# Moving loads, transforms and small matmuls between the steps of a fused Fourier-mixing and MLP kernel

## The chip, the cores and the metric

The kernel runs on one core of a Trainium2 chip. The metric is device time in microseconds (us), as the median of several executions. The granted clock is the share of TensorE's full clock that the profile shows as granted; 0.5 is called half clock here. Engines: PE is TensorE (PEld its weight loads), DVE is VectorE, ACT is ScalarE, POOL is GpSimd, and SP is SyncE, here used only to issue DMAs. Ratios are the mean time of one kernel's fast runs over the mean of the other's fast runs of the same rounds, so they are not quite the ratio of the medians quoted beside them. Verdicts are given at 2%.

## The reference

```python
# x: (8, 3008, 256) float32; w_in: (256, 2048); w_out: (2048, 256)
X = np.fft.fft(x, axis=1)          # along the sequence
X = np.fft.fft(X, axis=2).real     # along the channels, real part kept
h = X.reshape(24064, 256) @ w_in
out = (h * np.cos(h)) @ w_out
```

## The kernel before

The channel transform is folded into `w_in` once. The sequence transform of each batch is made of matmuls against constant matrices, after DVE has folded the 3008 rows by symmetry. Its result goes into ring buffers `Rr`, `Ir` and `Rb`. The MLP runs over 47 column tiles of 8 steps each, 376 steps in all; a batch lasts 47 steps. In each step PE makes `pp` and `pq` from the rings, DVE and ACT make `h`, and two steps later PE multiplies `h` into `po`. All other work (loads of the next batch, its folds, its transforms) is hung on steps by `at(step, fn)`.

Channel 128 of batches 1 to 7 is treated apart, which I call the one-channel stage. Two gathers fetch it, element by element, and seven batches are transformed together:

```python
    X0, X1 = Rr[0 : NB - 1, HALF + 32 :], Ir[0 : NB - 1, HALF + 32 :]

    def load_ext():                                  # the two gathers
        with nc.allow_non_contiguous_dma(reason="one channel"):
            for t, row in ((X0, 0), (X1, SEQ - 1536)):
                nc.sync.dma_start(
                    out=t,
                    in_=bass.AP(tensor=xt, offset=x.offset + (SEQ + row) * ND + 128,
                                ap=[[SEQ * ND, NB - 1], [ND, 1536], [1, 1]]))
```

A transform is six matmul instructions into two PSUM tiles, and a function that evacuates them with one ACT copy and two or three DVE operations:

```python
    def dft_pair(ri, kodd, stat, width, M, low, high, mid, banks=("da", "db")):
        pa = dps(banks[0])
        pb = dps(banks[1])
        # ... 3 matmuls into pb, 3 into pa ...
        def evacuate():
            bs = spool.tile([128, NE], FP, tag="bs", bufs=2, name="bs")
            pin(nc.scalar.copy(out=bs[0:M, 0:n], in_=pb[0:M, 0:n]))
            # ... DVE: sum and difference of bs and pa into the ring ...
        return evacuate
```

The schedule (`pin` keeps an operation in program order; everything else is ordered by the builder's scheduler):

```python
    at(2, lambda: dft_R(0, 1, EO)())          # matmuls and evacuation in one step
    at(5, lambda: dft_I(0, 1, EO)())
    at(8, lambda: dft_first(1, xb)())
    if NB > 1:
        at(1, load_ext)
        at(22, lambda: dft_ext(1, NB - 1, fold_ext()))   # whole one-channel stage
    for b in range(1, NB):
        s0 = (b - 1) * steps_b                            # steps_b = 47
        at(s0 + 1, lambda b=b: start_batch(b))            # issues the x loads
        for i in range(20):
            at(s0 + 5 + i, lambda i=i: state["ops"][FOLDS[i]]())
        at(s0 + 26, lambda b=b: dft_R(b, 0, state["EO"])())
        # ... dft_I at +29, dft_R at +32, dft_I at +35, spread_ext at +30 ...
    at(last - 8, spread4)
    at(last, middle_tokens)     # the 8 middle rows: 16 matmuls of 8 columns, MLP, 16 more
```

## Time and profile before

| | before |
|---|---|
| median (7 runs) | 2170.89 us |
| lowest, highest | 2168.28, 2178.56 us |
| profiled execution (not one of the 7) | 2167.05 us, span of the core 2165.3 us |
| PE, DVE, ACT busy | 99%, 84%, 41% |

These are lines of the page of the kernel before: the span, engine busy times with their share and count, the rows of PE's busy tenths and of the granted clock in 40 slices of 54 us, and the first line of the chain that ended last (the work that the end of the span waited for, followed back step by step).

```profile
span 2165.3 us, 24330 instructions
PE 2135.6 (99%) x9576; PEld 1809.5 (84%) x9576; DVE 1818.4 (84%) x2520; ACT 893.8 (41%) x896; POOL 109.6 (5%) x100
PE   8799999999999999999999999999999999999999
PEclk9899999999999999999999999999999999999999
PE 69%; DVE 21%; ACT 5%; DMA 1%; issue 1%; DVEq 0%; ACTq 0%
```

PE's 99% alone doesn't tell how much is to be won, since its passes overlap (those of `po` last 380 ns in the mean and start 216 ns apart) and a pass at half clock counts as busy all the same (four of them for 2.08 us below). I therefore used the start times of the passes. Each fp32 matmul instruction shows up as two passes, and a pass of 256 columns starts 216 ns after the one before it in the undisturbed stretches. What lies above that spacing (317 ns for 377 columns) is lost PE time. Summed per form it was 42 us in this execution. The largest piece, 18.4 us, lies between 76 and 99 us.

The PE timeline of the kernel before there (columns: start, length, engine, line, operation, tiles, shapes, count, and in brackets the idle time before with what ended it):

```profile
73.45 3.62 PE L555 MATMUL po<-w,h 128*128 128x256 f32 x16
87.92 2.08 PE L483 MATMUL pp<-Rr,Wc 128*128 128x256 f32 x4 [10.85 <-DVE pt L502]
89.78 1.91 PE L492 MATMUL pq<-Ir,Ws 127*128 127x256 f32 x4
```

Four passes took 1.03 us elsewhere and take 2.08 and 1.91 us here: after the gap the clock is at half (0.50 granted from 82.37 to 99.44 us). Here is the DVE instruction that ended the gap, from the timeline of all engines:

```profile
86.92 0.17 DVE L251 COPY e<-xl 128x6 f32<-128x6 f32 x1 [17.58 <-DMA xl<-in_x_dram]
```

`pt` stands behind this copy, the first fold of batch 1, in DVE's order, and starts right after it, at 87.00 us. And this is the queue of SyncE in the same stretch, where a length is that of the issuing instruction:

```profile
25.65 0.98 SPq L432 DMA_DIRECT2D Rr<-in_x_dram  x1
26.68 32.95 SPq L432 DMA_DIRECT2D Ir<-in_x_dram  x1
59.75 21.71 SPq L138 DMA_DIRECT2D xl<-in_x_dram  x1
81.56 0.37 SPq L140 DMA_DIRECT2D xl<-in_x_dram  x1
```

The gathers (`Rr` and `Ir` are their targets) stand ahead of the x tile (`xl`), and its issue isn't over until 81.5 us. The waits view of the kernel before (who waited for whom: us in total, times, longest):

```profile
DVE pt L502 <- PE pp L483: 38.5, 63, 3.9
PEld po L555 <- DVE h L534: 18.6, 42, 3.4
PE po L555 <- DVE h L534: 5.6, 9, 2.7
```

Last, the PE timeline of the one-channel stage of the kernel before:

```profile
189.45 5.50 PE L461 MATMUL da<-ident,Rr 7*128 7x7 f32 x24
195.26 3.62 PE L310 MATMUL db<-MC,xe 128*7 128x377 f32 x6 [0.32 <-ACT xe L469]
198.71 2.07 PE L310 MATMUL da<-MC,xe 128*7 128x377 f32 x6
```

Six passes of 377 columns took 3.62 us and then 2.07 us: the first six ran at half clock (0.50 granted from 191.60 to 198.43 us), right after 24 tiny passes.

### The profile page before, as it was taken

The numbers are of one execution on the slowest core, as the hardware profiler recorded it, in microseconds if no ns is written. First come the engines' busy times: TensorE is split into PE (matmuls) and PEld (weight loads), VectorE is DVE, ScalarE is ACT, GpSimd is POOL, SyncE is SP. The second block draws the span as 40 slices with busy tenths as digits, with TensorE's granted clock in tenths as the row PEclk, the third lists the DMA queues.
The fourth block names the chain that finished last, engine by engine and source line by source line (L and its number), as shares of the span: only waits on it lengthen the run. The fifth ranks groups of instructions, "written<-read, shape, count | busy, mean of one in ns | idle before, by whom it ended". The sixth has DMA issues, their size and how long they took to land.

```text
span 2165.3 us, 24330 instructions
## 1 busy us (share of the span) xinstructions
PE 2135.6 (99%) x9576; PEld 1809.5 (84%) x9576; DVE 1818.4 (84%) x2520; ACT 893.8 (41%) x896; POOL 109.6 (5%) x100
## 2 busy tenths in 40 slices
PE   8799999999999999999999999999999999999999
PEld 4587888888888888888888888888888888888887
DVE  5598788997889978898789987899778997888877
ACT  2243344443444434444344444444344443444434
POOL 4011000110001100010000200011000000000000
PEclk9899999999999999999999999999999999999999
DMA  8511000110011100110001100011000000000000
GB/s 255 46 35 41 25 10 24 54 34 11 10 40 40 35 10 10 53 36 24 10 10 58 47 10 11 23 56 32 10 10 25 20 10 10 10 17 14 10 11 20
DMA packets 63234, 66.02 MB, mean 30 GB/s; under 512 B 29576, under 2 KB 55944, under 8 KB 62607
## 3 DMA queue, kind: packets, MB, share of 16 engines
q1 hardware_dynamic: 56446, 51.86, 8.2%
q0 software_dynamic: 4608, 12.59, 2.1%
q8 instruction: 76, 1.25, 0.3%
q10 hardware_dynamic: 2066, 0.02, 0.1%
q14 instruction: 38, 0.31, 0.0%
HBM read 39.75 MB, written 24.69 MB: 30 GB/s over the span
## 4 chain that ended last, share of the span: by engine, by line
PE 69%; DVE 21%; ACT 5%; DMA 1%; issue 1%; DVEq 0%; ACTq 0%
PE po L555 43%; PE pp L483 10%; PE pq L492 10%; DVE r L528 6%; DVE h L534 5%; DVE pt L502 3%; ACT r L525 3%; DVE h L511 3%; DVE h L512 3%; PE db L310 2%; PE da L310 2%; DMA xl<-in_x_dram 1%; ACT r L531 1%; DVE o L238 1%; DVE e L238 0%
## 5 line engine op out<-in xcount | busy, mean ns | idle before, releaser
L555 PE MATMUL po<-w,h 128*128 128x256 f32 x6016 | 1366.7, 380 | 5.6 <-DVE h L534 5.6
L555 PEld LDWEIGHTS po<-w,h 128*128 128x128 f32 x6016 | 1138.8, 190 | 177.4 <-DVE h L534 18.6
L525 ACT ACTIVATE r<-h 128x1024 int32<-128x1024 f32 x377 | 396.9, 1053 | 626.9 <-DVE h L512 622.9
L531 ACT ACTIVATE r<-r,halfpi 128x1024 f32<-128x1024 f32 x377 | 432.4, 1147 | 540.9 <-DVE r L528 540.9
L528 DVE TENSOR_TENSOR r<-h,r 128x1024 f32<-128x1024 f32 x377 | 460.0, 1220 | 165.8 <-ACT r L525 162.6
L534 DVE SCALAR_TENSOR_TENSOR h<-h,r 128x1024 f32<-128x1024 f32 x377 | 459.2, 1218 | 53.0 <-ACT r L531 51.6
L483 PE MATMUL pp<-Rr,Wc 128*128 128x256 f32 x1504 | 390.6, 380 | 10.8 <-DVE pt L502 10.8
L492 PE MATMUL pq<-Ir,Ws 127*128 127x256 f32 x1504 | 388.9, 379 | 0.0
L502 DVE SCALAR_TENSOR_TENSOR pt<-Rb,wex,pp 128x256 f32<-128x256 f32 x752 | 330.7, 475 | 38.9 <-PE pp L483 38.5
L483 PEld LDWEIGHTS pp<-Rr,Wc 128*128 128x128 f32 x1504 | 285.9, 190 | 55.9 <-DVE pt L502 11.3
L492 PEld LDWEIGHTS pq<-Ir,Ws 127*128 127x128 f32 x1504 | 285.6, 190 | 41.1
L511 DVE TENSOR_TENSOR h<-pt,pq 128x512 f32<-128x512 f32 x376 | 258.0, 686 | 33.8 <-DVE pt L502 0.9
L512 DVE TENSOR_TENSOR h<-pt,pq 128x512 f32<-128x512 f32 x376 | 255.7, 680 | 0.0
L130 POOL DMA_INDIRECT xl<-in_x_dram,ix x96 | 109.4, 1140 | 1389.2 <-DVE o L238 1345.5
L576 ACT COPY ob<-po 128x512 f32<-128x512 f32 x94 | 54.3, 578 | 52.6 <-PE po L555 52.1
L310 PE MATMUL db<-MC,eo 128*128 128x377 f32 (+3 forms) x186 | 65.0, 486 | 2.0 <-DVE eo L238 2.0
L310 PE MATMUL da<-MC,eo 128*128 128x377 f32 (+3 forms) x186 | 64.7, 483 | 0.0
L310 PEld LDWEIGHTS da<-MC,eo 128*128 128x128 f32 (+1 forms) x186 | 35.7, 192 | 24.4 <-issue 1.2
L310 PEld LDWEIGHTS db<-MC,eo 128*128 128x128 f32 (+1 forms) x186 | 35.4, 191 | 20.4 <-DVE eo L238 2.8
L251 DVE COPY e<-xl 128x6 f32<-128x6 f32 x32 | 5.4, 167 | 33.1 <-DMA xl<-in_x_dram 33.1
L238 DVE TENSOR_TENSOR o<-xl 128x762 f32<-128x762 f32 x32 | 30.3, 948 | 0.0
L238 DVE TENSOR_TENSOR e<-xl 128x762 f32<-128x762 f32 x32 | 30.3, 946 | 0.0
(65 smaller groups left out, 218.4 us busy)
## 6 DMA issues: line engine op xcount, KB each, us to landing
out_dram<-ob SPq DMA_DIRECT2D x158, 128.0 KB
xl<-in_x_dram SPq DMA_DIRECT2D x16, 768.0 KB
MC<-dft_mats SPq DMA_DIRECT2D x4, 1131.0 KB
Rb<-r SPq DMA_DIRECT2D x4, 752.0 KB
h<-in_moe_w_in_dram SPq DMA_DIRECT2D x4, 512.0 KB
w<-in_moe_w_out_dram SPq DMA_DIRECT2D x1, 2048.0 KB
xl<-in_x_dram,ix POOLq DMA_INDIRECT x96
out_dram<-ob SPq DMA_DIRECT2D x10, 112.0 KB
```

What stands on the lines that cost most here:

```text
L130: nc.gpsimd.indirect_dma_start(out=L[j][:, m * ND : (m + 1) * ND], out_offset=None, in_=xflat, in_offset=bass.IndirectOffsetOnAxis(ap=ix[: ...
L310: nc.tensor.matmul(ps[0:M, 0:n], lhsT=stat[:, m * width : m * width + M], rhs=MC[ri, kodd][:, c : c + n], start=(t == 0), stop=(t == 2),)
L483: nc.tensor.matmul(pp[:, i * TW : (i + 1) * TW], lhsT=Wc[:, f * 128 : (f + 1) * 128], rhs=Rr[:, pos : pos + TW], start=True, stop=True,)
L492: nc.tensor.matmul(pq[:, i * TW : (i + 1) * TW], lhsT=Ws[0:127, f * 128 : (f + 1) * 128], rhs=Ir[:, pos : pos + TW], start=True, stop=True,)
L502: nc.vector.scalar_tensor_tensor(out=pt[:, i * TW : (i + 1) * TW], in0=Rb[:, pos : pos + TW], scalar=wex[:, f : f + 1], in1=pp[:, i * TW : ...
L511: nc.vector.tensor_tensor(out=h[:, 0:512], in0=pt, in1=pq, op=ALU.add)
L512: nc.vector.tensor_tensor(out=h[:, 512:1024].rearrange("p (f c) -> p f c", f=2)[:, :, ::-1], in0=pt.rearrange("p (f c) -> p f c", f=2), in ...
L525: nc.scalar.activation(out=k, in_=h[:, 0:n], func=AF.Copy, bias=0.25, scale=1.0)
L528: nc.vector.tensor_tensor(out=r[:, 0:n], in0=h[:, 0:n], in1=k, op=ALU.subtract)
L531: nc.scalar.activation(out=r[:, 0:n], in_=r[:, 0:n], func=AF.Sin, bias=halfpi, scale=TWO_PI)
L534: nc.vector.scalar_tensor_tensor(out=h[:, 0:n], in0=h[:, 0:n], scalar=TWO_PI, in1=r[:, 0:n], op0=ALU.mult, op1=ALU.mult,)
L555: nc.tensor.matmul(T.po[sg][:, gr * ND : (gr + 1) * ND], lhsT=g[:, c : c + 128], rhs=w2[:, f * ND : (f + 1) * ND], start=(f == 0 and gr == 0),
```

## The change

The intent is to take lumps out of the schedule. There are five parts:

1. The gathers are issued after the x tiles of batch 1 (step 2 instead of 1, and pinned).
2. Folds and transforms of all batches come two steps later.
3. Each transform is evacuated one step after its matmuls.
4. The one-channel stage is cut into a fold, four pieces of transposes, and two transforms three steps apart.
5. The 16 small matmuls of the middle tokens are spread, two to a step.

The diff, cut to its core:

```diff
     def load_ext():
 ...
-                nc.sync.dma_start(
+                pin(
+                    nc.sync.dma_start(
 ...
+    def at_dft(step, fn):
+        def first():
+            state["evacuate"] = fn()
+        at(step, first)
+        at(step + 1, lambda: state["evacuate"]())
 ...
-    at(2, lambda: dft_R(0, 1, EO)())
+    at_dft(2, lambda: dft_R(0, 1, EO))
 ... (the same at 5 and 8)
-        at(1, load_ext)
-        at(22, lambda: dft_ext(1, NB - 1, fold_ext()))
+        at(2, load_ext)
+        at(21, fold_ext)
+        for part in range(4):
+            at(22 + part, lambda part=part: turn_ext(part))
+        at_dft(30, lambda: dft_ext(0))
+        at_dft(33, lambda: dft_ext(1))
+        at(34, store_ext)
 ...
-        for i in range(20):
-            at(s0 + 5 + i, lambda i=i: state["ops"][FOLDS[i]]())
-        at(s0 + 26, lambda b=b: dft_R(b, 0, state["EO"])())
+        for i, key in enumerate(FOLDS):
+            at(s0 + 7 + i, lambda key=key: state["ops"][key]())
+        at_dft(s0 + 28, lambda b=b: dft_R(b, 0, state["EO"]))
 ... (the same for 29, 32, 35 -> 31, 34, 37; spread_ext two steps later, five for batch 1)
+    for part in range(8):
+        at(last - 8 + part, lambda part=part: middle_first(part))
     at(last, middle_tokens)
```

More of the change, by code (lines that the diff above doesn't have):

```diff
@@ L183 @@
     wex = cpool.tile([128, NF], FP, tag="wex")
+    state = {}
     Rr = cpool.tile([128, RING], FP, tag="Rr")
@@ L389, in dft_I, with dft_ext, low, high @@
         return dft_pair(1, kodd, EO[2 + kodd], 127, 127, low, high, None, **kw)
-    def dft_ext(b0, nb, ext):
-        rx = spool.tile([NB, HALF], FP, tag="xl3", bufs=1, name="rx")
-        rx4 = spool.tile([NB, 1], FP, tag="rx4", bufs=1, name="rx4")
-        for kodd in range(2):
-            def low(op, a, z, kodd=kodd):
-                op(rx[0:nb, kodd * RUN + a : kodd * RUN + z], a, z)
-            def high(op, a, z, kodd=kodd):
-                top = kodd * RUN + (RUN - 1 if kodd else RUN)
-                op(rx[0:nb, top - a : top - z : -1], a, z)
-            dft_pair(
-                0, kodd, ext[kodd], nb, nb, low, high,
-                lambda hi: hi(rx4[0:nb, :], 0, 1),
-            )()
-        nc.sync.dma_start(out=r128_dr[b0 : b0 + nb, :], in_=rx[0:nb, :])
+    def dft_ext(kodd):
+        nb = NB - 1
+        if kodd == 0:
+            state["rx"] = spool.tile([nb, HALF], FP, tag="xl3", bufs=1, name="rx")
+            state["rx4"] = spool.tile([nb, 1], FP, tag="rx4", bufs=1, name="rx4")
+        rx, rx4 = state["rx"], state["rx4"]
+        def low(op, a, z):
+            op(rx[:, kodd * RUN + a : kodd * RUN + z], a, z)
+        def high(op, a, z):
+            top = kodd * RUN + (RUN - 1 if kodd else RUN)
+            op(rx[:, top - a : top - z : -1], a, z)
+        return dft_pair(
+            0, kodd, state["ext"][kodd], nb, nb, low, high,
+            lambda hi: hi(rx4, 0, 1),
+        )
+    def store_ext():
+        nc.sync.dma_start(out=r128_dr[1:NB, :], in_=state["rx"])
         nc.sync.dma_start(
-            out=r4_dr[:, b0 : b0 + nb].rearrange("o b -> b o"), in_=rx4[0:nb, :]
+            out=r4_dr[:, 1:NB].rearrange("o b -> b o"), in_=state["rx4"]
         )
@@ L431, in load_ext @@
             for t, row in ((X0, 0), (X1, SEQ - 1536)):
-                nc.sync.dma_start(
-                    out=t,
-                    in_=bass.AP(
-                        tensor=xt,
-                        offset=x.offset + (SEQ + row) * ND + 128,
-                        ap=[[SEQ * ND, NB - 1], [ND, 1536], [1, 1]],
-                    ),
+                pin(
+                    nc.sync.dma_start(
+                        out=t,
+                        in_=bass.AP(
+                            tensor=xt,
+                            offset=x.offset + (SEQ + row) * ND + 128,
+                            ap=[[SEQ * ND, NB - 1], [ND, 1536], [1, 1]],
+                        ),
+                    )
                 )
@@ L455, in fold_ext, with turn_ext @@
         pin(nc.vector.memset(em[:, n:768], 0.0))
+    def turn_ext(part):
         nb = NB - 1
-        ps = dps("da")
-        for i, t in enumerate((ep, em)):
-            for m in range(6):
-                c = (i * 6 + m) * nb
-                pin(nc.tensor.matmul(
-                    ps[:, c : c + nb],
-                    lhsT=t[:, m:768:6],
-                    rhs=ident[0:nb, 0:nb],
-                    start=True,
-                    stop=True,
-                ))
+        ep, em = X0[:, 0:768], X0[:, 768:1536]
+        if part == 0:
+            state["xe_ps"] = dps("da")
+        ps = state["xe_ps"]
+        for j in range(3 * part, 3 * part + 3):
+            i, m = divmod(j, 6)
+            pin(nc.tensor.matmul(
+                ps[:, j * nb : (j + 1) * nb],
+                lhsT=(ep, em)[i][:, m:768:6],
+                rhs=ident[0:nb, 0:nb],
+                start=True,
+                stop=True,
+            ))
+        if part < 3:
+            return
         xe = spool.tile([128, 12 * nb], FP, tag="xe", bufs=1, name="xe")
         pin(nc.scalar.copy(out=xe, in_=ps[:, 0 : 12 * nb]))
-        return [xe[:, 0 : 6 * nb], xe[:, 6 * nb :]]
+        state["ext"] = [xe[:, 0 : 6 * nb], xe[:, 6 * nb :]]
     class Tile:
@@ L599, in store, with middle_first @@
                 j += n
-    def middle_tokens():
-        pm = dps("da")
-        for f in range(NF):
+    def middle_first(part):
+        if part == 0:
+            state["pm"] = dps("da")
+        pm = state["pm"]
+        for f in range(2 * part, 2 * part + 2):
             nc.tensor.matmul(
@@ L611, in middle_tokens @@
             )
+    def middle_tokens():
+        pm = state["pm"]
         n = NF * NB
@@ L660 @@
     steps_b = HALF * 8 // TW
-    state = {}
+    def at_dft(step, fn):
[3 more added lines that the diff above has]
+        at(step + 1, lambda: state["evacuate"]())
     def start_batch(b):
         state["EO"], state["ops"] = fold_x(load_x(b))
-    at(2, lambda: dft_R(0, 1, EO)())
-    at(5, lambda: dft_I(0, 1, EO)())
-    at(8, lambda: dft_first(1, xb)())
+    at_dft(2, lambda: dft_R(0, 1, EO))
+    at_dft(5, lambda: dft_I(0, 1, EO))
+    at_dft(8, lambda: dft_first(1, xb))
     if NB > 1:
-        at(1, load_ext)
-        at(22, lambda: dft_ext(1, NB - 1, fold_ext()))
+        at(2, load_ext)
[5 more added lines that the diff above has]
+        at(34, store_ext)
     for b in range(1, NB):
@@ L674 @@
         at(s0 + 1, lambda b=b: start_batch(b))
-        for i in range(20):
-            at(s0 + 5 + i, lambda i=i: state["ops"][FOLDS[i]]())
-        at(s0 + 26, lambda b=b: dft_R(b, 0, state["EO"])())
-        at(s0 + 29, lambda b=b: dft_I(b, 0, state["EO"])())
-        at(s0 + 32, lambda b=b: dft_R(b, 1, state["EO"])())
-        at(s0 + 35, lambda b=b: dft_I(b, 1, state["EO"])())
-        at(s0 + 30, lambda b=b: spread_ext(b))
+        for i, key in enumerate(FOLDS):
+            at(s0 + 7 + i, lambda key=key: state["ops"][key]())
+        at_dft(s0 + 28, lambda b=b: dft_R(b, 0, state["EO"]))
+        at_dft(s0 + 31, lambda b=b: dft_I(b, 0, state["EO"]))
+        at_dft(s0 + 34, lambda b=b: dft_R(b, 1, state["EO"]))
+        at_dft(s0 + 37, lambda b=b: dft_I(b, 1, state["EO"]))
+        at(s0 + (35 if b == 1 else 32), lambda b=b: spread_ext(b))
     total = n_tiles * 8
```

## The prediction

> **What bounds the kernel now.** TensorE. The busy table gives PE 99% of 2165.3 us, DVE 84%, ACT 41%. In the timeline most steps repeat every 5.18 us, which is 24 passes, so one starts every 216 ns. Start-to-start time above the median of a pass's own form sums, over all 9576 passes, to only 42 us of lost PE time: 8.4 us in the first 40 us, 18.4 us between 76 and 99 us, about 3 us between 189 and 199 us, and 12 us in pieces of 0.2 to 0.7 us. Only those can be won by moving work; no engine gets more instructions.
>
> **The large gap.** The waits view has one DVE wait of 17.58 us, ending at 86.92 us: the first copy of the batch-1 fold, on the landing of the x tile. The SyncE queue shows why: the two one-channel gathers (7 x 1536 elements of 4 bytes each) are issued at 25.65 and 26.68 us, the second issue lasts 32.95 us, and that of the x tile behind it 21.71 us. [...] from 55 to 80 us some 2500 four-byte packets per 5 us pass, and next to no bytes. Behind it PE idles 10.85 us (pp waits for pt) and 2.73 us (po for h), and the granted clock is 0.5 from 82.4 to 99.4 us, costing the remaining 4.8 us. [...]
>
> **What the change does there.** The x tiles of batch 1 now stand ahead of the gathers on the queue, and the folds start two steps (10 us) later. The x issue should come near 35 us, when its buffer comes free, and land by 50 to 60 us; the first fold wants it near 75 us. The gathers, some 55 us long (estimate from this trace), are wanted only at step 21 (about 150 us). So the DVE wait, the PE gap and the slow clock go: -18.4 us, all on the critical path.
>
> **The one-channel stage.** Before: 24 tiny transposes (5.5 us) and four transforms run in one block at 189 to 204 us; PE waits 0.46 + 0.32 us, the clock is 0.5 from 191.6 to 198.4 us and six passes take 0.63 us instead of 0.32. Spread out, the clock should stay at 1: -3 us. The 5.5 us of transposes stay.
>
> **The rest.** Splitting each transform from its evacuation frees ACT waits (3.7 us at most) that PE hardly feels: 0 to -2 us. The middle-token matmuls (3.5 us) only move: 0. In fold steps DVE has about 5.7 us of work per 5.18 us step; the 5 us of one-channel folding at step 21 now has less PE work right behind it to let DVE catch up: up to +2 us of new PE waits.
>
> **Sum.** -18.4 - 3 - 1 + 1 = -21: predicted 2149 us, range 2141 to 2158. Chances: faster by over 2% (2127.5, more than all avoidable loss) 0.01, within 2% 0.98, slower 0.01.
>
> **What would show it.** Right: no DVE wait above 3 us on the x tile after 40 us; no idle PE near 76 to 92 us; clock digits 9 in the second to fourth slice; span near 2144. Wrong: if the gathers still delay the x tile or the first output stores (ACT waits for an output buffer near 120 us); if DVE falls behind at 150 to 180 us and PE waits there for h; if a transform waits over 1 us for the evacuation of the last (single buffers).

## The result and the profile after

| | before | after |
|---|---|---|
| median | 2170.89 us (15 runs) | 2142.39 us (6 runs) |
| lowest, highest | 2165.78, 2178.80 us | 2140.79, 2144.34 us |
| span of the profiled execution | 2165.3 us | 2140.7 us |
| ratio, 95% interval | | 0.9863 [0.9847, 0.988] |

The change is 1.4% faster. Two things in the table need an explanation beyond the median: the scatter shrank from 13 us to 3.6 us, and the medians lie 28.5 us apart but the profiled spans only 24.6 us. The lines of the page that answer to those of before:

```profile
span 2140.7 us, 24296 instructions
PE 2126.8 (99%) x9576; PEld 1807.6 (84%) x9576; DVE 1821.0 (85%) x2520; ACT 893.6 (42%) x896; POOL 111.0 (5%) x100
PE   8999999999999999999999999999999999999999
PEclk9999999999999999999999999999999999999999
PE 98%; DVE 1%; POOL 0%; DMA 0%; issue 0%; ACT 0%; DVEq 0%; ACTq 0%
```

PE does the same 9576 passes, but the chain that ended last now runs over PE for 98% of the span, where it ran over DVE for 21% before. The SyncE queue of the changed kernel:

```profile
34.76 0.36 SPq L138 DMA_DIRECT2D xl<-in_x_dram  x1
35.22 0.37 SPq L140 DMA_DIRECT2D xl<-in_x_dram  x1
35.64 0.97 SPq L440 DMA_DIRECT2D Rr<-in_x_dram  x1
36.66 27.70 SPq L440 DMA_DIRECT2D Ir<-in_x_dram  x1
96.32 0.82 SPq L611 DMA_DIRECT2D out_dram<-ob  x2
```

The first output stores are issued at 96.32 us, after the gathers (99% of their packets had started by 86.5 us), so they aren't held up either.

The first fold of batch 1 finds its data without a wait, and PE, in its own timeline of the changed kernel, goes on through that stretch at full speed (four passes in 1.03 us):

```profile
83.49 0.17 DVE L253 COPY e<-xl 128x6 f32<-128x6 f32 x1
```

```profile
77.89 1.03 PE L499 MATMUL pp<-Rr,Wc 128*128 128x256 f32 x4
78.75 1.03 PE L508 MATMUL pq<-Ir,Ws 127*128 127x256 f32 x4
```

The waits of the changed kernel: PE hardly waits for `h` any more, and DVE, now ahead, waits 95.6 us instead of 38.5 for the next `pp`.

```profile
DVE pt L518 <- PE pp L499: 95.6, 138, 3.1
PEld po L571 <- DVE h L550: 5.2, 18, 0.9
PE po L571 <- DVE h L550: 0.5, 1, 0.5
```

The one-channel stage is cut, and six passes of a transform in it take 2.07 us:

```profile
167.75 2.83 PE L475 MATMUL da<-ident,Rr 7*128 7x7 f32 x12
170.51 3.72 PE L571 MATMUL po<-w,h 128*128 128x256 f32 x16
174.16 1.49 PE L475 MATMUL da<-ident,Rr 7*128 7x7 f32 x6
...
211.44 2.07 PE L312 MATMUL db<-MC,xe 128*7 128x377 f32 x6
```

To see where the 24.6 us came from I compared the start of the first `po` pass of each step in the two traces. The lead of the changed kernel over the kernel before:

| at the start of step | lead, us | what lies before it |
|---|---|---|
| 0 | -0.98 | start-up (6.83 us at half clock, against 3.41 us in before) |
| 6 | 17.37 | the stall at 76 to 99 us: 18.35 us |
| 46 | 17.99 | rest of batch 0, with the one-channel stage: 0.6 us |
| 329 | 24.57 | batches 1 to 6, the short waits: 6.6 us |
| 375 | 24.56 | the middle tokens and the end: 0 |

The prediction had 18.4, 2 (3 less 1 of new waits), 1 and 0 for the last four rows.

### The profile page after: what moved, and what is told of

It is laid out like the page before. It is cut to its first block, busy times and chain, and to the rows that moved or that the text cites. A ratio compares the mean times of both kernels' runs of the same rounds, so it can differ in the third digit from the quotient of the medians.

```text
span 2140.7 us, 24296 instructions
## 1 busy us (share of the span) xinstructions
PE 2126.8 (99%) x9576; PEld 1807.6 (84%) x9576; DVE 1821.0 (85%) x2520; ACT 893.6 (42%) x896; POOL 111.0 (5%) x100
## 3 DMA queue, kind: packets, MB, share of 16 engines
q8 instruction: 76, 1.25, 0.2%
q10 hardware_dynamic: 2066, 0.02, 0.1%
## 4 chain that ended last, share of the span: by engine, by line
PE 98%; DVE 1%; POOL 0%; DMA 0%; issue 0%; ACT 0%; DVEq 0%; ACTq 0%
PE po L571 60%; PE pp L499 15%; PE pq L508 15%; PE db L312 3%; PE da L312 3%; POOL xl L130 0%; PE db L647 0%; DMA xl<-in_x_dram,ix 0%; PE da L475 0%; DVE r L544 0%; PE po L312 0%; DVE h L550 0%; ACT r L541 0%; DVE pt L518 0%; PE da L623 0%
## 5 line engine op out<-in xcount | busy, mean ns | idle before, releaser
L518 DVE SCALAR_TENSOR_TENSOR pt<-Rb,wex,pp 128x256 f32<-128x256 f32 x752 | 332.7, 476 | 98.4 <-PE pp L499 95.6
L253 DVE COPY e<-xl 128x6 f32<-128x6 f32 x32 | 5.5, 172 | 15.3 <-DMA xl<-in_x_dram 13.7
```

The costliest lines, as they stand in the source:

```text
L518: nc.vector.scalar_tensor_tensor(out=pt[:, i * TW : (i + 1) * TW], in0=Rb[:, pos : pos + TW], scalar=wex[:, f : f + 1], in1=pp[:, i * TW : ...
```

## The experiments

Theory 1: the order on the SyncE queue makes the stall, and nothing else of it matters. Its rival: the two later steps make the difference. For the 6.6 us of short waits, theory A says that the split of transform and evacuation removes them, theory B that the place of the folds does. "Short waits" in the table is lost PE time by start-to-start times in batches 1 to 6, counting passes that came over 5 ns late; the kernel before has 8.8 us of it.

| kernel | median, us | ratio to before, 95% | profiled span | short waits | x-tile wait of the first fold |
|---|---|---|---|---|---|
| before | 2170.89 | | 2165.3 | 8.8 | 17.6 |
| the changed kernel | 2142.39 | 0.9863 [0.9847, 0.988] | 2140.7 | 2.2 | none |
| e1_order | 2152.51 | 0.9914 [0.9899, 0.9929] | 2151.6 | 8.6 | none |
| e2_late | 2158.07 | 0.9945 [0.9917, 0.9972] | 2154.0 | 7.2 | 8.5 |
| e3_split | 2163.89 | 0.9965 [0.9949, 0.9981] | 2167.4 | 2.9 | 21.6 |
| e4_spread | 2170.96 | 1.0007 [0.9984, 1.0029] | 2169.9 | 7.8 | 19.2 |
| e_osm | 2144.01 | 0.9863 [0.9835, 0.989] | 2142.1 | 2.9 | none |
| u_split | 2146.57 | 0.99 [0.9884, 0.9917] | 2144.8 | 7.7 | none |
| u_mid | 2144.4 | 0.9888 [0.9872, 0.9905] | 2142.4 | 2.1 | none |
| u_late | 2142.86 | 0.9859 [0.9831, 0.9887] | 2142.6 | 2.9 | none |
| u_order | 2147.69 | 0.9882 [0.9857, 0.9907] | 2145.4 | 2.0 | 3.7 |
| w_warm | 2141.53 | 0.986 [0.9831, 0.9889] | 2139.3 | 2.0 | none |

Two more kernels, d_before and d_after, follow below. All twelve experiment kernels gave correct results. Rows of one call (the four e1 to e4; u_mid, u_split and the two d; the last four) share their runs of before; the medians of before were 2170.11, 2169.51 and 2170.53 us in the three calls. Its times ran up to 2182.86 us in the third, which widens those intervals. The changed kernel was timed in a call of its own, so a difference of under 1 us between its median and another's is not read as one.

### e1_order: the queue order alone

```diff
-        at(1, load_ext)
+        at(2, load_ext)      # and both gathers pinned
```

In the built program this leaves the order on PE, DVE and ACT the same, line for line.

> The kernel before with one thing changed: the x tiles of batch 1 stand ahead of the two four-byte gathers on the SyncE queue. The order of instructions on PE, DVE and ACT is the same as before, line for line. Theory 1 (the queue order makes the whole stall at 76 to 99 us): the DVE wait of 17.6 us on the x tile is gone, the folds two steps earlier than in the changed kernel still find their data, the span is 17 to 19 us under before, near 2147, and the times scatter by under 5 us instead of 13, because the scatter of before is the length of the gathers. The small PE waits of batches 1 to 6 (8.8 us by start-to-start times in before) stay. Theory 2 (the later folds are what matters, the queue order only helps): a good part of the wait remains, over 5 us, and the gain is under 10 us.

It gained 17.6 us in the median. The trace shows no wait on the x tile at the fold, a lead over before of 17.4 us at step 6, and the same short waits as before. Its times lay within 1.8 us. Theory 1 holds: one line of queue order is the whole stall, and most of the scatter went with it (1.8 us). The x tile's issue in e1_order, and the line of its waits view for the x tile, whose two waits both lie in the start-up, before 20 us:

```profile
34.69 0.36 SPq L138 DMA_DIRECT2D xl<-in_x_dram  x1
DVE e L251 <- DMA xl<-in_x_dram: 13.2, 2, 9.1
```

Its span was only 13.7 us under that of before, less than the 17 to 19 us expected, since 3.3 us of the lead were lost at the middle tokens (see u_mid).

### e2_late and u_late: the two later steps, alone and left out

```diff
 # e2_late, against before: all of a batch's folds, transforms and spread two steps later
-            at(s0 + 5 + i, ...)
+            at(s0 + 7 + i, ...)
 # u_late, against the changed kernel: back to 5, with the one-channel transforms moved along
```

> The kernel before with only the folds, transforms and spread of batches 1 to 7 two steps later; the gathers still stand ahead of the x tile. Theory 1: the x tile still lands near 87 us, the first fold asks for it some 10 us later, so 10 to 14 of the 18.4 us stall go and some 4 to 8 us remain; the wide scatter remains. If in addition the small waits of batches 1 to 6 come from where the folds lie, their 8.8 us fall to about 2 us and the span is near 2165 - 12 - 6 = 2147; if they come from the unsplit transforms they stay at about 8 us and the span is near 2153.

> The changed kernel with the folds and transforms of all batches two steps earlier, as before (the one-channel transforms and the spread move with them, to keep the transforms apart). With the queue order mended the x tiles land by 55 us and the first fold asks for them at 70 us or later, so theory 1 gives no DVE wait on them and a time within 2 us of the changed kernel: 2140 to 2144. If the two later steps are needed, a DVE wait on the x tile of several us comes back near 70 us.

With the gathers still first, the later folds shortened the wait on the x tile from 17.6 to 8.5 us. PE still lost 8.7 us there (75 to 125 us), a little over the 4 to 8 us expected. The scatter stayed at 15 us (2150.93 to 2166.24). The short waits fell only to 7.2 us, so theory B fails. With the queue order mended, going back two steps cost nothing that can be told apart: 2142.86 us. The later steps are a second remedy for the same stall, and superfluous beside the first. The first fold of batch 1 in e2_late:

```profile
90.49 0.17 DVE L251 COPY e<-xl 128x6 f32<-128x6 f32 x1 [8.47 <-DMA xl<-in_x_dram]
```

### u_order: the gathers first again, all else changed

```diff
 # against the changed kernel
-        at(2, load_ext)      # pinned
+        at(1, load_ext)      # not pinned
```

> The changed kernel with the gathers again ahead of the x tiles; the order on PE, DVE and ACT stays line for line that of the changed kernel. As with the later folds alone, where 8.7 us of lost PE time were left between 75 and 125 us, I expect a DVE wait on the x tile of 5 to 12 us near 85 us, 5 to 10 us lost on PE with the clock at 0.5 after it, a median of 2147 to 2153, and a scatter of more than 6 us, since the end of the gathers sets it. If the order on the queue had nothing to do with it, the time stays at 2142.

The median went up by 5.3 us against the changed kernel's, within the expectation, and the PE order is again the same line for line. But the wait was 3.7 us (line below), less than the 5 to 12 us that I expected, and the scatter was only 2.0 us, where I expected over 6. I had carried over the number of e2_late. In both, DVE asks for the x tile at 82 us; it landed at 85.9 us here and at 90.5 us there. That landing varied between 85.9 and 90.5 us over the five traces with the gathers first (without the third gather). Why the six times of u_order nevertheless lie so close together I can't say. Taking the two results together: the queue order was worth 17.4 us alone and 5.3 us when removed last. Both are right. When two parts of a change cure one stall, leaving one out shows little. The first fold in u_order:

```profile
85.91 0.17 DVE L253 COPY e<-xl 128x6 f32<-128x6 f32 x1 [3.68 <-DMA xl<-in_x_dram]
```

### d_before and d_after: one more gather

```diff
-            for t, row in ((X0, 0), (X1, SEQ - 1536)):
+            for t, row in ((X0, 0), (X1, SEQ - 1536), (Rb[0 : NB - 1, HALF + 32 :], 0)):
```

The third gather goes to a part of `Rb` that is free then, and its data are not used.

> The kernel before with a third one-channel gather of the same size, in front of the x tile. If the gathers in front of the x tile make the stall, half as many four-byte packets again add half the 55 us that they take: the x tile lands near 114 us, the DVE wait grows from 17.6 to 42 to 48 us, and the time grows by 22 to 30 us, to near 2196. If the stall had another cause (the DMA engines' load from the other inputs, the indirect loads), it grows by under 10 us.

> The changed kernel with the same third gather. The x tiles are ahead of it, the gathers then end near 115 us instead of 87, and are wanted only at step 21, after 150 us. If they are off the critical path, as I predicted, the time stays within 2 us of the changed kernel, 2141 to 2145, and only the first output stores move, from 96 to about 110 us. If the gathers still hold something up, it grows by 5 us or more.

d_before had a median of 2191.6 us, ratio 1.0114 [1.0096, 1.0131], and d_after 2143.38 us, ratio 0.9884 [0.9867, 0.99]. The SyncE queue of d_before:

```profile
25.59 35.02 SPq L432 DMA_DIRECT2D Ir<-in_x_dram  x1
60.66 21.97 SPq L432 DMA_DIRECT2D Rb<-in_x_dram  x1
82.75 21.68 SPq L138 DMA_DIRECT2D xl<-in_x_dram  x1
```

and its waits:

```profile
DVE e L251 <- DMA xl<-in_x_dram: 52.5, 3, 38.8
PE pp L483 <- DVE pt L502: 32.0, 1, 32.0
```

The wait on the x tile grew by 21.2 us, from 17.6 to 38.8 us, which is under the 42 to 48 us I gave, and the time by 22 us, the low end of my range. I had taken half of 55 us, counted from the issue; the packets themselves pass from 34.7 to 82.0 us, and the third gather moved that end to 103.7 us, by 21.7 us. In d_after the same gather cost PE nothing that its trace shows: no PE gap after the start-up, and the traces of d_after and the changed kernel stay within 0.1 us of each other from step 30 to the end. The gathers are off the critical path there, with room for at least 10,752 more elements. They still hold up what stands behind them: the issue of the first output store, at 94.70 us, lasted 22.35 us; PE shows no gap for it.

### e3_split and u_split: the evacuation a step later, alone and left out

```diff
 # e3_split, against before
-    at(2, lambda: dft_R(0, 1, EO)())
+    at_dft(2, lambda: dft_R(0, 1, EO))    # likewise for all main transforms
 # u_split, against the changed kernel
-        at(step + 1, lambda: state["evacuate"]())
+        at(step, lambda: state["evacuate"]())
```

> The kernel before with only the main transforms split from their evacuations by a step. Theory A (the split removes the small PE waits of batches 1 to 6): they fall from 8.8 us to 2 or 3 us, and the stall of 18 us stays, so the span is near 2159. Theory B (they come from the fold steps' place): they stay at about 8 us and the span is within 2 us of 2165.

> The changed kernel with each transform evacuated in its own step again (main and one-channel ones). Theory A (the split removes the small PE waits): those of batches 1 to 6 rise from 2.2 us to 6 to 9 us, the span to 2145 to 2148. Theory B (the split does nothing, the place of the folds does): they stay near 2 us and the span within 1 us of 2140.7.

Theory A holds both ways: the split alone takes the short waits from 8.8 to 2.9 us, and leaving it out brings them back to 7.7 us. Medians moved by 6.2 us and 4.2 us. The waits of u_split look like those of before:

```profile
PEld po L571 <- DVE h L550: 14.1, 39, 0.9
PE po L571 <- DVE h L550: 2.4, 8, 0.5
```

(I had expected a span of 2159 us for e3_split. Its profiled execution, at 2167.4 us, was its slowest, with a wait of 21.6 us on the x tile instead of 17.6 and the slow clock at the middle tokens; its six times lie from 2161.30 to 2169.19 us.)

The surprising part is where the waits are. They aren't at the transforms, but in the first fold steps of the next batch. The split changed the order that the builder lays down for DVE far beyond the transforms (284 of the 2520 DVE instructions of its trace stand in another place than in that of before; so do some of PE and ACT). In both kernels a fold step asks more of DVE than the step lasts: 4.75 us for the step's own six operations and 0.95 us for the fold, against 5.18 us. So the margin by which `h` is ready before `po` shrinks. From the traces, that margin at steps 5 to 12 of batch 3, in us:

```
step              5     6     7     8     9    10    11    12
before         1.34  0.06  0.63  0.06  0.63  0.06  0.99  0.06
e3_split       2.66  1.40  1.88  1.40  1.88  0.45  1.71  0.29
```

A margin of 0.06 us means that PE was waiting: at the four such steps of before in this table the `po` pass started 55 to 415 ns late, at the other four on time. In steps without folds the margin runs through a cycle of three steps, for batch 2 at steps 38 to 40 it is 1.05, 2.25, 1.72 us in before and 1.99, 1.25, 2.45 us in e3_split: the same cycle, on average 0.2 us larger and shifted by a step. That the split causes the change is shown by the two runs. That it acts through DVE's order is argued from these margins, and why this order leaves DVE further ahead isn't known: it is a property of what the scheduler made, and I ran nothing that separates the order from the split.

### e4_spread: the one-channel stage in pieces

```diff
 # against before
-        at(22, lambda: dft_ext(1, NB - 1, fold_ext()))
+        at(20, fold_ext)
+        for part in range(4):
+            at(21 + part, lambda part=part: turn_ext(part))
+        at_dft(27, lambda: dft_ext(0))
+        at_dft(30, lambda: dft_ext(1))
+        at(31, store_ext)
```

> The kernel before with only the one-channel stage in pieces (fold at step 20, four pieces of transposes, two split transforms). My prediction gave this 3 us, the clock staying at 1 there, less up to 2 us of new waits. Expected: no clock of 0.5 near 190 us, the six passes of 0.63 us back at 0.32, a gain of 0 to 3 us over before, the stall at 76 to 99 us untouched. Rival: it gains nothing or loses, since the transposes between ordinary passes cost PE as much as the slow clock did.

No gain is shown: the ratio's interval includes 1, though at 3.5 us faster to 6.3 us slower it is too wide to exclude the 0 to 3 us expected. The trace shows a small loss. The six passes are back at 1.91 us instead of 3.45 us, but the trace is still at half clock for 3.41 us, from 183.4 us, after 12 passes of two pieces (six transposes) that the scheduler put back to back, and PE falls behind by 0.7 us between steps 18 and 30. Across all kernels with the stage in one block, six of six profiled executions had the clock at half there, for 6.8 us in five; of the eight with it in pieces, five had it for 3.4 us and three not at all. So the pieces shorten the slow clock, which is worth less than the 3 us of my prediction, and they don't end it in every execution. The changed kernel's profiled execution was one of the three without it; the one of w_warm, with the same pieces, had it.

### u_mid: the middle tokens in one step again

```diff
 # against the changed kernel
-        at(last - 8 + part, lambda part=part: middle_first(part))
+        at(last, lambda part=part: middle_first(part))
```

> The changed kernel with all 32 middle-token passes of 8 columns again in one step. My prediction gave their spreading 0. New theory: a block of 3.6 us of 8-column passes [...] the clock is 0.5 for 6.8 us after it and 3.3 us are lost (seen in three of the four variants just run, not in the one profiled execution of before). Expected: a clock of 0.5 near 2060 us and a span and median 2 to 4 us above the changed kernel, 2143 to 2146. Rival (the place of these passes is worth nothing): same as the changed kernel, 2140 to 2143, no 0.5 there.

The median rose by 2.0 us and the span by 1.7 us, all of it lost at the middle tokens in the trace. The median alone proves little: u_mid has only four times, and d_after, which should equal the changed kernel, lies 1.0 us under it. What happens is best seen in e1_order, which has the same block and, in its profiled execution, a longer slow stretch after it:

```profile
2063.47 4.16 PE L607 MATMUL da<-R,Wc 128*128 128x8 f32 x32
2067.49 2.05 PE L485 MATMUL pp<-Rr,Wc 128*128 128x256 f32 x4
2069.33 1.91 PE L494 MATMUL pq<-Ir,Ws 127*128 127x256 f32 x4
```

The changed kernel, four passes at a time:

```profile
2014.45 0.51 PE L623 MATMUL da<-R,Wc 128*128 128x8 f32 x4
2014.82 1.11 PE L499 MATMUL pp<-Rr,Wc 128*128 128x256 f32 x4
```

The profile shows no idle time of PE in either. Yet after 32 passes of 8 columns the granted clock is at half (0.76 in the mean of 2062 to 2076 us in e1_order) and four ordinary passes take 2.05 us. In e1_order this cost 3.3 us (its lead over before fell from 17.0 to 13.7 us there). Of seven profiled executions with the block, four showed it (e1_order, e3_split, e4_spread, and u_mid, where the mean is 0.83 from 2056 to 2066 us, so 3.4 us at half), while before, e2_late and d_before didn't; of the seven with the passes spread, none did. My prediction read one execution of before, which happened to be one without it, and called the move worth 0.

What decides between the executions isn't shown.

### e_osm: three parts alone

This is before with the queue order, the split of the main transforms, and the spread middle tokens; without the later folds and the pieces of the one-channel stage.

> The kernel before with three parts of the change only: the x tiles ahead of the gathers, the main transforms split from their evacuations, the middle-token passes spread. Left out: the two later steps for the folds, and the one-channel stage in pieces. If the three explain the gain, the profiled span is 2165.3 - 17.4 (queue order) - 5.7 (split) + 0 to 1.5 (the block of the one-channel stage with its slow clock, which the change lacks) = 2142 to 2144, and the median 2143 to 2146. If the later folds or the pieces of the one-channel stage matter by themselves, it stays above 2147.

2144.01 us, and a span of 2142.1 us: three of the five parts give the whole gain but 1.6 us (2144.01 against 2142.39 us), and that rest isn't clear of the scatter.

### w_warm: an attempt to go further

In the changed kernel PE sits idle for 3.4 us before the first transform, and the clock is at half from 25.6 to 32.4 us. I put 8 matmuls there whose results nobody reads:

```diff
     fold_weights()
+    idle = dps("da")
+    for _ in range(8):
+        pin(nc.tensor.matmul(idle[:, 0:256], lhsT=CC[:, 0:128], rhs=CC[:, 0:256], start=True, stop=True))
```

> The changed kernel with 8 extra matmuls (16 passes, 3.5 us, results not used) after the folding of the weights, where PE sits idle for 3.6 us before the first transform. If the clock of 0.5 between 25.6 and 32.4 us comes from that idle time and lies on the critical path, it goes, the first transforms take 0.32 us a pass instead of 0.63, and the time falls by 1.5 to 3 us, to 2139.5 to 2141. If PE is not what bounds that stage, or the extra passes end after the data of the first transform arrive, the gain is under 1 us.

The clock stayed at full there (1.00 in the mean of 22 to 48 us, against 0.87 in the changed kernel). The first six passes of the first transform took 2.17 us instead of 4.14 us, and the first `po` pass came 2.9 us earlier. PE timeline of w_warm, then of the changed kernel:

```profile
22.43 3.62 PE L662 MATMUL da<-CC 128*128 128x256 f32 x16
26.51 2.17 PE L312 MATMUL db<-MC,eo 128*128 128x377 f32 x6 [0.47 <-DVE eo L240]
```

```profile
26.50 4.14 PE L312 MATMUL db<-MC,eo 128*128 128x377 f32 x6 [3.43 <-DVE eo L240]
```

But 1.7 us was given back at 168 us, where this execution, unlike the changed kernel's, was at half clock for 3.4 us in the one-channel stage. Its median is 0.9 us under the changed kernel's, not the 1.5 to 3 us expected; its five times lie between 2139.93 and 2146.23 us, and its ratio of 0.986 can't be told from the changed kernel's 0.9863. It isn't shown to be a better kernel; what is shown, in one trace, is that the start-up has 2.9 us to give.

## Why the prediction was right or wrong

The time (2142.39 us) lies inside the predicted range of 2141 to 2158 us, 1.4 us above its lower end and 6.6 us under the value named, and "within 2%" was right. That it lies inside is partly luck: the split was worth 5.6 us more than the sum allowed, and the one-channel stage 1.4 us less. Point by point:

- **The bound.** PE was the bound and only its lost time could be won. Right: the lost time by the same sum fell from 41.9 to 19.9 us.
- **The stall, -18.4 us.** Right, in size and in cause. The x tile was issued at 34.76 us (predicted near 35), no fold waited for it, and 18.35 us went. e1_order, and the added gather of d_before and d_after, show the cause. The prediction gave two causes at once, the queue order and the later folds; the first alone suffices, and the second isn't needed.
- **The one-channel stage, -3 us, and new waits of up to +2 us.** Too large. The profiled pair shows 0.6 us for that stretch, and e4_spread shows no gain alone. Twelve passes (six transposes) back to back were followed by 3.41 us at half clock in five of eight executions.
- **"Splitting each transform from its evacuation frees ACT waits ... that PE hardly feels: 0 to -2 us."** This is the step that was mis-sized: the term measured 6.6 us in the profiled pair, and 5.9 us in the short waits of e3_split. I looked for the effect at the transforms, where ACT waited. It lies in the fold steps of the next batch, probably through the DVE order that the scheduler lays down. I had seen the 12 us of small pieces, but not asked which part of the change would reach them.
- **"The middle-token matmuls only move: 0."** Right for the profiled pair and wrong for four of the seven profiled executions with the block: there the clock was at half after it, which cost 1.7 us (u_mid) to 3.3 us (e1_order).
- **The sum.** I took its terms from a profiled execution of 2167.05 us, 3.8 us under the median of before, and subtracted them from that median. The difference of the medians is larger than that of the spans because that execution was a fast one of a scattering kernel; what made it fast is read from other traces. Its gathers had all but ended (99% of their packets started) at 82.0 us; in e3_split and e4_spread, with the same order, at 84.2 and 84.4 us. And it lacked the slow clock at the middle tokens.

Beside the prediction, the traces show this of the gathers and of the clock. In before about 21,600 four-byte packets pass on the SyncE queue between 24 and 110 us, for 21,504 gathered elements, so about one for each. The gathers took about 47 us (1% to 99% of the packets started between 34.7 and 82.0 us), or 2.2 ns per element (an estimate from these figures). The instruction that issues the x tile lasted 21.71 us behind them in before and 0.36 us in front of them in the changed kernel. The stretches at half clock, but for the one at the end of each execution, lasted 3.41, 17.07 and 6.83 us in before and 6.83 us in the changed kernel. The last of these in before, from 191.60 us, began during 24 passes of 7 by 7, and the one at the middle tokens of e1_order came with 32 passes of 8 columns; PE had no idle time before either. Why some executions had such a stretch and others not, these runs don't show.

## What to carry to other kernels

Order a DMA queue by when the data are wanted: two gathers of single elements, only 42 KB each, held up the x tile behind them until 86.92 us here, and DVE's order carried that wait to PE. Don't judge a change on one profiled execution of a scattering kernel: the one of before had the shortest stall of the three traces with its schedule of folds (17.6 us against 19.2 and 21.6), and lacked a slow clock that four of seven executions showed. Where a scheduler orders the engines, look for the effect of a move in the whole order and not just at the place of the move; and where two parts of a change cure the same stall, try each alone and not only left out.
